# A gated linear attention with a mixer behind it: the attention runs one chunk ahead, the mixing is cut into small units, and the weights are loaded before the second batch

## The chip, the cores and the metric

The kernel runs on one core of one Trainium2 chip. The metric is the device time of one execution in microseconds (us); the kernel before took 243.04, 241.78 and 242.86 us in three runs, median 242.86. Engines are named as in the profile: PE (matrix unit; its weight loads stand apart as PEld), DVE (vector engine), ACT (activation engine), POOL (GpSimd), SP (the queue that issues plain DMAs). DMAs that convert a type are issued on POOL's queue.

## The reference

```python
# 4 batches, 8 heads, 768 steps, head width 48
f = 1 / (1 + exp(-f_logit))
for t in range(768):                                   # attention
    state = f[:, :, t, :, None] * state + k[:, :, t] (outer) v[:, :, t]
    y[:, :, t] = q[:, :, t] @ state
x = y.transpose(0, 2, 1, 3).reshape(4, 768, 384)
h  = relu(x^T @ w_tok1) @ w_tok2                       # 768 -> 256 -> 768, over the steps
u  = x + h^T
out = u + relu(u @ w_ch1) @ w_ch2                      # 384 -> 1536 -> 384, over the channels
```

All inputs and the output are fp32; both kernels use bf16 for matmuls and fp32 for sums.

## The kernel before, in words

**Attention.** The 768 steps of a batch are 6 chunks of 128. Per chunk (b, c) the log gates, split in two bf16 parts Lhi and Llo, are summed over the steps by two matmuls with a triangular matrix (`attn_front`, L154 and L156, 512 columns, into `ps_S`); eight matmuls of one column (L161, L163) give the sum over the whole chunk. ACT makes G = exp(-S), Gi = exp(S) and `glast`. DVE makes qh = q·G and kh = k·Gi. PE transposes both against an identity (L182 into `ps_AT[0]`, L184 into `ps_AT[1]`), ACT and DVE copy them to `qkT`, PE makes the scores of 8 heads (L191, into the same two banks), DVE masks them (`AmT`, L200, L201). PE makes y from `AmT` and v (L204) and adds qkT·state (L210); four matmuls of 96 columns (L215) make k·v of a pair of heads, of whose 2x2 blocks only the diagonal ones are used, so that DVE adds them to `state` in two instructions of 48 partitions, multiplies by `glast` and copies two blocks to `state_bd`. ACT writes y twice, as fp32 `x_nat` and bf16 `x_bf`.

**Mixing.** For a whole batch, in 6 slices: tok (w_tok1 12 matmuls, Relu to `h1T`; w_tok2 12 matmuls, DVE adds to `u_nat`, ACT casts to `u_bf`), utr (18 transposes, three DVE copies to `uT`), three slices of ch1 (24 units of 3 matmuls of 384 columns, each drained by a Relu on DVE or ACT to `zT`), and ch2 (6 units of 12 matmuls of 384 columns, one DVE add, one output DMA).

**Order.** The slices of batch b-1 are emitted inside the chunks of batch b, one slice a chunk, between the scores and the mask. The gates of batch b+1 (exp, ln, a copy to Lhi, a subtraction to Llo, each over the whole batch) are emitted one step a chunk. The mixing of batch 3 has no attention beside it. Eight PSUM tiles have fixed roles: five for attention (`ps_S`, `ps_AT` twice, `ps_y`, `ps_dg`), three rotate for the mixing. A scheduler then sets the order on each engine; it moves instructions across the places where they are written, and each engine runs its own list in order.

**Loads.** In this order: batch 0 chunk by chunk (f on SP; q, k, v on POOL's queue, 18 DMAs), batch 1 whole (q, k, v on POOL's queue, f on SP), the four weights (POOL's queue). Batch b+2 is loaded into the buffers of batch b when these are free.

Of the kernel before, what the change touches and what calls it, by code (L numbers as in the profile page):

```python
# [16 lines left out]
def kernel(  # L18
# [39 lines left out]
    w_ch1 = st([128, 3, DCH], BF16, "w_ch1")
    w_ch2 = st([128, 12, DM], BF16, "w_ch2")

    def load_weights():
        nc.gpsimd.dma_start(out=w_tok1, in_=moe_w_tok1.rearrange("(kt p) n -> p kt n", p=128))
        nc.gpsimd.dma_start(out=w_tok2, in_=moe_w_tok2.rearrange("(kt p) n -> p kt n", p=128))
        nc.gpsimd.dma_start(out=w_ch1, in_=moe_w_ch1.rearrange("(kt p) n -> p kt n", p=128))
        nc.gpsimd.dma_start(out=w_ch2, in_=moe_w_ch2.rearrange("(kt p) n -> p kt n", p=128))

    q_sb = [st([128, H, NCH, D], BF16, f"q_sb{i}") for i in range(2)]
    k_sb = [st([128, H, NCH, D], BF16, f"k_sb{i}") for i in range(2)]
    v_sb = [st([128, H, NCH, D], BF16, f"v_sb{i}") for i in range(2)]
# [4 lines left out]
    def load_batch_inputs(b, c0=0, c1=NCH):
        i = b % 2
        if (c0, c1) == (0, NCH):
            nc.gpsimd.dma_start(out=q_sb[i], in_=q[b].rearrange("h (c t) d -> t h c d", t=C))
            nc.gpsimd.dma_start(out=k_sb[i], in_=k[b].rearrange("h (c t) d -> t h c d", t=C))
            nc.gpsimd.dma_start(out=v_sb[i], in_=v[b].rearrange("h (c t) d -> t h c d", t=C))
            nc.sync.dma_start(out=f_sb[i], in_=f_logit[b].rearrange("h (c t) d -> t h c d", t=C))  # L80
# [11 lines left out]
    G = [st([128, H, 64], BF16, f"G{i}") for i in range(2)]
    Gi = [st([128, H, 64], BF16, f"Gi{i}") for i in range(2)]
    qh = [st([128, H, 64], BF16, f"qh{i}") for i in range(2)]
    kh = [st([128, H, 64], BF16, f"kh{i}") for i in range(2)]
    qkT = [st([128, 8, 128], BF16, f"qkT{i}") for i in range(2)]
    AmT = [st([128, 8, 128], BF16, f"AmT{i}") for i in range(2)]
    glast = st([128, HP], FP32, "glast")
    state = st([128, HP, D], FP32, "state")
    state_bd = st([128, HP, 2 * D], BF16, "state_bd")  # L100
    x_nat = [st([128, NCH, DM], FP32, f"x_nat{i}") for i in range(2)]
    x_bf = [st([128, NCH, DM], BF16, f"x_bf{i}") for i in range(2)]
# [6 lines left out]
    for tl in (*Lhi, *Llo):
        nc.vector.memset(tl[:, :, :, D:64], 0.0)  # L110
    nc.vector.memset(state_bd, 0.0)

    ps_S = pt([128, 512], FP32, "ps_S")
    ps_AT = [pt([128, 4, 128], FP32, f"ps_AT{p}") for p in range(2)]
    ps_y = pt([128, H, D], FP32, "ps_y")
    ps_dg = pt([128, HP, 2 * D + 1], FP32, "ps_dg")

    h1T = st([128, 2, DM], BF16, "h1T")
    u_nat = st([128, NCH, DM], FP32, "u_nat")
    u_bf = st([128, NCH, DM], BF16, "u_bf")  # L120
    uT = st([128, 3, S], BF16, "uT")
    zT = st([128, 12, S], BF16, "zT")
# [253 lines left out]
```

## Time and profile before

| What | Value |
|---|---|
| median of three runs | 242.86 us |
| the profiled execution's own time | 242.51 us |
| its span in the trace | 240.4 us |
| PE / PEld / DVE / ACT / POOL busy | 183.6 / 111.5 / 152.1 / 137.2 / 40.1 us |
| DMA | 19.93 MB, 91539 packets, 80896 of them under 512 B |
| MATMULs seen, 128x384 | ch1 288, ch2 288 |

The span is the time between the first and the last instruction seen; the execution's own time is 2.1 us longer. Shares over the whole span mix an early part, in which little runs but DMAs, with later parts in which PE is nearly always busy. The tables below are therefore cut at the first ch1 matmul of batch 0 and at the first w_tok1 matmul of batches 1, 2 and 3.

### The profile page before, as it was taken

The numbers are of one execution on the slowest core, as the hardware profiler recorded it, in microseconds if no ns is written. First come the engines' busy times: TensorE is split into PE (matmuls) and PEld (weight loads), VectorE is DVE, ScalarE is ACT, GpSimd is POOL, SyncE is SP. The second block draws the span as 40 slices with busy tenths as digits, with TensorE's granted clock in tenths as the row PEclk, the third lists the DMA queues.
The fourth block names the chain that finished last, engine by engine and source line by source line (L and its number), as shares of the span: only waits on it lengthen the run. The fifth ranks groups of instructions, "written<-read, shape, count | busy, mean of one in ns | idle before, by whom it ended". The sixth has DMA issues, their size and how long they took to land.

```text
span 240.4 us, 4273 instructions
## 1 busy us (share of the span) xinstructions
PE 183.6 (76%) x1673; PEld 111.5 (46%) x1688; DVE 152.1 (63%) x341; ACT 137.2 (57%) x262; POOL 40.1 (17%) x39
## 2 busy tenths in 40 slices
PE   0413376103858999999999999999999999989993
PEld 0201253001535555566565555666556556546661
DVE  4323769300965999995489998637999872444221
ACT  5479999900697765870376777008776710556300
POOL 9823910821302100150300000000000000000000
PEclk9999999999965999999999999999999999999999
DMA  8999999999999900099490000121000002100022
GB/s 113 147 185 151 163 158 137 174 144 198 208 182 137 103 3 0 3 85 174 135 104 0 3 1 3 65 100 35 0 3 0 3 33 102 64 0 0 8 107 85
DMA packets 91539, 19.93 MB, mean 83 GB/s; under 512 B 80896, under 2 KB 91136, under 8 KB 91520
## 3 DMA queue, kind: packets, MB, share of 16 engines
q0 software_dynamic: 77168, 10.23, 78.3%
q1 hardware_dynamic: 14352, 9.44, 18.4%
q8 instruction: 13, 0.21, 0.4%
q14 instruction: 6, 0.05, 0.1%
HBM read 25.17 MB, written 4.72 MB: 124 GB/s over the span
## 4 chain that ended last, share of the span: by engine, by line
PE 34%; DVE 26%; DMA 15%; issue 9%; ACT 8%; POOL 7%; DVEq 0%; POOLq 0%
DMA q_sb_77<-in_q_dram 6%; DMA w_tok_73<-in_moe_w_tok_dram 6%; PE ps_moe_135 L298 5%; PE ps_moe_133 L298 5%; PE ps_moe_134 L298 5%; PE ps_moe_133 L280 3%; DMA out_dram<-out_sb_132 3%; DVE zT L285 3%; PE ps_moe_134 L280 3%; PE ps_moe_135 L280 3%; DVE u_nat L256 2%; DVE qkT_98 L186 2%; DVE AmT_99 L200 2%; DVE uT L270 2%; DVE state L225 2%
## 5 line engine op out<-in xcount | busy, mean ns | idle before, releaser
L298 PEld LDWEIGHTS <-zT 128*128 128x128 bf16 x288 | 27.7, 98 | 18.3
L280 PEld LDWEIGHTS <-w_ch_75 128*128 128x128 bf16 x288 | 26.5, 97 | 19.9 <-issue 4.5
L280 PE MATMUL ps_moe_133<-uT,w_ch_75 128*128 128x384 bf16 x96 | 22.9, 325 | 1.4 <-DVE uT L270 0.5
L280 PE MATMUL ps_moe_135<-uT,w_ch_75 128*128 128x384 bf16 x96 | 22.6, 325 | 0.8 <-DVE zT L285 0.5
L280 PE MATMUL ps_moe_134<-uT,w_ch_75 128*128 128x384 bf16 x96 | 22.2, 325 | 0.5 <-DVE zT L285 0.3
L220 ACT ACTIVATE x_nat_105<-ps_y 128x384 f32<-128x384 f32 x12 | 6.0, 499 | 24.8 <-PE ps_y L210 24.2
L298 PE MATMUL ps_moe_134<-w_ch_76,zT 128*128 128x384 bf16 x96 | 17.3, 326 | 0.0
L200 DVE TENSOR_TENSOR AmT_100<-ps_AT_122,tri_bf 128x512 bf16<-128x512 f32 x12 | 8.3, 688 | 14.2 <-PE ps_AT_123 L191 14.0
L298 PE MATMUL ps_moe_135<-w_ch_76,zT 128*128 128x384 bf16 x96 | 17.1, 326 | 0.0
L298 PE MATMUL ps_moe_133<-w_ch_76,zT 128*128 128x384 bf16 x96 | 17.1, 326 | 0.0
L287 ACT ACTIVATE zT<-ps_moe_134 128x384 bf16<-128x384 f32 x22 | 10.9, 496 | 8.0 <-PE ps_moe_134 L280 7.8
L161 PE MATMUL ps_dg<-ones_bf,Lhi_85 128*128 128x1 bf16 x40 | 3.5, 166 | 13.5 <-ACT Lhi_85 L143 6.7
L287 ACT ACTIVATE zT<-ps_moe_135 128x384 bf16<-128x384 f32 x22 | 11.0, 500 | 4.9 <-PE ps_moe_135 L280 4.8
L220 ACT ACTIVATE x_nat_104<-ps_y 128x384 f32<-128x384 f32 x12 | 5.8, 486 | 13.9 <-PE ps_y L210 13.9
L247 PE MATMUL ps_moe_134<-x_bf_106,w_tok_73 128*128 128x384 bf16 x6 | 2.5, 452 | 14.1 <-DMA w_tok_73<-in_moe_w_tok_dram 12.2
L247 PEld LDWEIGHTS <-w_tok_73 128*128 128x128 bf16 x48 | 4.6, 105 | 17.9 <-DMA w_tok_73<-in_moe_w_tok_dram 12.4
L287 ACT ACTIVATE zT<-ps_moe_133 128x384 bf16<-128x384 f32 x20 | 10.0, 500 | 4.3 <-PE ps_moe_133 L280 4.2
L224 DVE TENSOR_TENSOR state<-state,ps_dg 48x192 f32<-48x192 f32 x20 | 6.8, 342 | 8.5 <-ACT qkT_98 L185 4.9
L257 ACT ACTIVATE u_bf<-u_nat 128x384 bf16<-128x384 f32 x24 | 11.0, 519 | 1.8 <-DVE u_nat L256 1.6
L200 DVE TENSOR_TENSOR AmT_99<-ps_AT_122,tri_bf 128x512 bf16<-128x512 f32 x12 | 8.2, 685 | 6.0 <-PE ps_AT_123 L191 5.7
L175 ACT ACTIVATE glast<-ps_dg 128x4 f32<-128x4 f32 x20 | 3.6, 178 | 14.1 <-DVE state L227 12.7
L191 PE MATMUL ps_AT_122<-qkT_97 48*128 48x128 bf16 x48 | 5.1, 232 | 7.3 <-ACT qkT_97 L185 5.5
(149 smaller groups left out, 470.3 us busy)
## 6 DMA issues: line engine op xcount, KB each, us to landing
out_dram<-out_sb_131 SPq DMA_DIRECT2D x12, 192.0 KB, 1.9
out_dram<-out_sb_132 SPq DMA_DIRECT2D x12, 192.0 KB, 1.9
f_sb_83<-in_f_logit_dram SPq DMA_DIRECT2D x6, 192.0 KB, 5.7
q_sb_78<-in_q_dram POOLq DMA_DIRECT2D x2, 576.0 KB, 12.6
k_sb_80<-in_k_dram POOLq DMA_DIRECT2D x2, 576.0 KB, 18.2
v_sb_82<-in_v_dram POOLq DMA_DIRECT2D x2, 576.0 KB, 11.6
w_ch_75<-in_moe_w_ch_dram POOLq DMA_DIRECT2D x1, 1152.0 KB, 20.3
w_ch_76<-in_moe_w_ch_dram POOLq DMA_DIRECT2D x1, 1152.0 KB, 24.9
```

The lines of the kernel that those rows point to most:

```text
L186: nc.vector.tensor_copy(qkT[i][:, 4:8, :], ps_AT[1])
L191: nc.tensor.matmul(ps_AT[par][:, hp, :], lhsT=qkT[i][rows, 4 + hp, :], rhs=qkT[i][rows, hp, :], start=True, stop=True)
L200: nc.vector.tensor_tensor(AmT[i][:, 0:4, :], ps_AT[0], tb4, ALU.mult)
L220: nc.scalar.activation(x_nat[ib][:, c, :], yflat, AF.Copy, bias=0.0, scale=1.0)
L224: nc.vector.tensor_tensor(state[0:D], state[0:D], ps_dg[0:D, :, 0:D], ALU.add)
L225: nc.vector.tensor_tensor(state[64:64 + D], state[64:64 + D], ps_dg[64:64 + D, :, D:2 * D], ALU.add)
L247: nc.tensor.matmul(pm[:, 0:DM], lhsT=w_tok1[:, kt, rt * 128:(rt + 1) * 128], rhs=x_bf[ib][:, kt, :], start=(kt == 0), stop=(kt == NCH - 1))
L257: nc.scalar.activation(u_bf[:, stt, :], u_nat[:, stt, :], AF.Copy, bias=0.0, scale=1.0)
L280: nc.tensor.matmul(pm[:, 0:384], lhsT=w_ch1[:, kt, cc * 128:(cc + 1) * 128], rhs=uT[:, kt, th * 384:(th + 1) * 384], start=(kt == 0), stop ...
L285: nc.vector.tensor_scalar(dst, pm[:, 0:384], 0.0, None, ALU.max)
L287: nc.scalar.activation(dst, pm[:, 0:384], AF.Relu, bias=0.0, scale=1.0)
L298: nc.tensor.matmul(pm[:, 0:DM], lhsT=zT[:, kt, tt * 128:(tt + 1) * 128], rhs=w_ch2[:, kt, :], start=(kt == 0), stop=(kt == 11))
```

## The change

The kernel is written anew with the same arithmetic; what differs:

- **Attention ahead.** `attn_chunk` becomes `front` (gate sums to qh, kh), `scores` (transposes to AmT), `update` (state) and `readout` (y). Step n emits scores of chunk n+1, update of n, front of n+2, readout of n.
- **Mixing units.** The mixing of a batch is 44 units (2 tok1, 6 tok2, 6 utr, 24 ch1, 6 ch2) with weights; a credit spreads them evenly over four places in each of the 6 steps of the next batch.
- **PSUM.** Mixing takes 3 tiles of tag "mix", attention takes 5 rotating tiles of tag "att".
- **Compact state.** Eight matmuls of 48 columns write k·v of each head to its own partitions, so that `state` is one add and one multiply over 128 partitions; `state` and `state_bd` are doubled. S has 384 columns in place of 512, with the chunk sums in the same bank.
- **Engines.** Lhi is a second Ln on ACT, not a copy. Beyond batch 0, Llo, `x_bf` (now cast from `x_nat`), `u_bf` and the two `state_bd` copies go to POOL; in batch 0 they are on DVE. `uT` is copied by ACT, one block of steps at a time (6 of 128x384). 10 of 24 ch1 units drain on DVE, against 8 before. One activation table set is loaded at the start.
- **Loads.** f of batch 0, then q, k, v of batch 0 by chunks; the weights; then f, q, k, v of batch 1, f on POOL's queue too.

```diff
-        nc.tensor.matmul(ps_S, lhsT=tri_bf, rhs=hi_c.rearrange("t h dd -> t (h dd)"), ...)
+        nc.tensor.matmul(Sv, lhsT=tri_bf, rhs=Lhi[i][:, c, :, 0:D], start=True, stop=False)   # Sv = pS[:, 0:384]
...
-            for hp in range(HP):
-                nc.tensor.matmul(ps_dg[:, hp, 0:2 * D], lhsT=kb[:, hp, :],
-                                 rhs=v_sb[ib][:, 2 * hp:2 * hp + 2, c, :], ...)
+        for h in range(H):
+            hp, par = h // 2, h % 2
+            nc.tensor.matmul(pd[par * 64:par * 64 + 64, hp * D:(hp + 1) * D], lhsT=kh[j][:, h, :],
+                             rhs=v_sb[i][:, h, c, :], start=True, stop=True)
...
+            nc.vector.tensor_tensor(s, state[1 - j], pdv, ALU.add)
+            nc.vector.tensor_tensor(s, s, g, ALU.mult)
+        eng = nc.gpsimd if b else nc.vector
+        eng.tensor_copy(state_bd[j][0:D, :, 0:D], s[0:D])
+        eng.tensor_copy(state_bd[j][64:64 + D, :, D:2 * D], s[64:64 + D])
...
-        nc.scalar.activation(x_bf[ib][:, c, :], yflat, AF.Copy, bias=0.0, scale=1.0)
+        (nc.gpsimd if b else nc.vector).tensor_copy(x_bf[i][:, c, :], x_nat[i][:, c, :])
...
-                nc.scalar.activation(u_bf[:, stt, :], u_nat[:, stt, :], AF.Copy, bias=0.0, scale=1.0)
+            (nc.gpsimd if b else nc.vector).tensor_copy(u_bf[:, tt, :], u_nat[i][:, tt, :])
...
+        nc.scalar.activation(fb, fb, AF.Exp, bias=0.0, scale=-1.0)
+        nc.scalar.activation(Lhi[i][:, c0:c1, :, 0:D], fbc, AF.Ln, bias=1.0, scale=1.0)
+        nc.scalar.activation(fb, fb, AF.Ln, bias=1.0, scale=1.0)
+        eng = nc.gpsimd if b else nc.vector
+        eng.tensor_tensor(Llo[i][:, c0:c1, :, 0:D], fbc, Lhi[i][:, c0:c1, :, 0:D], ALU.subtract)
...
-    load_batch_inputs(1)
-    load_weights()
+    for w, src in ((w_tok1, moe_w_tok1), (w_tok2, moe_w_tok2), (w_ch1, moe_w_ch1), (w_ch2, moe_w_ch2)):
+        nc.gpsimd.dma_start(out=w, in_=src.rearrange("(kt p) n -> p kt n", p=128))
+    load_f(1, nc.gpsimd)
+    load_qkv(1)
...
+        def mix():
+            nonlocal credit
+            credit += per_step                  # the sum of the units' weights / 24
+            while prev and credit >= prev[0][0] / 2:
+                w, fn = prev.pop(0)
+                credit -= w
+                fn()
+        if n + 1 < len(steps):
+            scores(*steps[n + 1])
+        mix()
+        update(b, c)
+        mix()
+        if n + 2 < len(steps):
+            front(*steps[n + 2])
+        mix()
+        readout(b, c)
+        mix()
+        if b + 1 < B and 1 <= c <= 3:
+            gates(b + 1, 2 * (c - 1), 2 * c)
```

**POOL's queue, at the end of the first loads.** Before (buffers 77, 79, 81 hold batches 0 and 2; 78, 80, 82 batches 1 and 3):

```order
L89 DMA v_sb_81<-in_v_dram 128x8x48
L77 DMA q_sb_78<-in_q_dram 128x48x48
L78 DMA k_sb_80<-in_k_dram 128x48x48
L79 DMA v_sb_82<-in_v_dram 128x48x48
L62 DMA w_tok_73<-in_moe_w_tok_dram 128x6x256
L63 DMA w_tok_74<-in_moe_w_tok_dram 128x2x768
L64 DMA w_ch_75<-in_moe_w_ch_dram 128x3x1536
L65 DMA w_ch_76<-in_moe_w_ch_dram 128x12x384
L77 DMA q_sb_77<-in_q_dram 128x48x48
```

With the change (78, 80, 82 hold q, k, v of batches 0 and 2; 79, 81, 83 and f_sb_85, Lhi_87, Llo_89 belong to batches 1 and 3):

```order
L278 DMA w_tok_75<-in_moe_w_tok_dram 128x2x768
L278 DMA w_ch_76<-in_moe_w_ch_dram 128x3x1536
L278 DMA w_ch_77<-in_moe_w_ch_dram 128x12x384
L110 DMA f_sb_85<-in_f_logit_dram 128x48x48
L118 DMA q_sb_79<-in_q_dram 128x48x48
L118 DMA k_sb_81<-in_k_dram 128x48x48
L118 DMA v_sb_83<-in_v_dram 128x48x48
L131 TENSOR_TENSOR Llo_89<-f_sb_85,Lhi_87 128x16x48 x3
L118 DMA q_sb_78<-in_q_dram 128x48x48
L118 DMA k_sb_80<-in_k_dram 128x48x48
L118 DMA v_sb_82<-in_v_dram 128x48x48
L207 CAST state_bd_106<-state_104 48x4x48
```

The weights moved ahead of batch 1, f of batch 1 came in from SP's queue, and POOL now has work of the attention between its DMAs: the three parts of Llo of batch 1 stand behind the issue of v of batch 1, and the first state copy of batch 1 behind the loads of batch 2.

**DVE, where the first mixing begins** (batch 0's tok and utr, beside the first chunks of batch 1). Before:

```order
L256 TENSOR_TENSOR u_nat<-x_nat_104,ps_moe_133 128x384
L256 TENSOR_TENSOR u_nat<-x_nat_104,ps_moe_134 128x384
L256 TENSOR_TENSOR u_nat<-x_nat_104,ps_moe_135 128x384
L201 TENSOR_TENSOR AmT_99<-ps_AT_123,tri_bf 128x512
L230 CAST state_bd<-state 48x4x48
L270 COPY uT<-ps_moe_133 128x768
L270 COPY uT<-ps_moe_134 128x768
```

With the change:

```order
L202 TENSOR_TENSOR state_104<-pd,gl_102 128x192
L228 TENSOR_TENSOR u_nat_113<-x_nat_108,pm 128x384
L150 TENSOR_TENSOR qh_94<-q_sb_79,G_90 128x8x48
L229 CAST u_bf<-u_nat_113 128x384
L151 TENSOR_TENSOR kh_96<-k_sb_81,Gi_92 128x8x48
L228 TENSOR_TENSOR u_nat_113<-x_nat_108,pm 128x384 x2
L229 CAST u_bf<-u_nat_113 128x384 x2
```

DVE gained the casts to `u_bf` in this batch and lost the copies to `uT`; in the later batches the casts are POOL's. The rows of `u_nat` now stand around the qh and kh of chunk (1, 2). On PE the first matmul of chunk (1, 0), with Lhi of batch 1, stands ahead of the readout of chunk (0, 4).

More of the change, by code (lines that the diff above doesn't have):

```diff
@@ L92 @@
[L92 to L100, printed above, removed]
@@ L104, in blk @@
+    h1T = st([128, 2, DM], BF16, "h1T")
+    u_nat = two([128, NCH, DM], FP32, "u_nat")
+    u_bf = st([128, NCH, DM], BF16, "u_bf")
+    uT = st([128, 3, S], BF16, "uT")
+    zT = st([128, NCC, S], BF16, "zT")
+    out_sb = two([128, DM], FP32, "out_sb")
+    for tl in (*Lhi, *Llo):
+        nc.vector.memset(tl[:, :, :, D:64], 0.0)
+    for tl in (*qh, *kh):
+        nc.vector.memset(tl[:, :, D:64], 0.0)
+    for tl in state_bd:
+        nc.vector.memset(tl, 0.0)
     def blk(ap3):
         return ap3.rearrange("t (hp par) dd -> t hp (par dd)", par=2)
-    for tl in (*qh, *kh, *G, *Gi):
-        nc.vector.memset(tl[:, :, D:64], 0.0)
@@ L109 @@
[L109 to L122, printed above, removed]
```

386 lines of the change are left out of this document (171 added, 215 removed).

## The prediction

> **What bounds the kernel now.** I read the page's slices first, then busy time by stage, the chain of waits, the longest waits, the DMA issues.
>
> ```profile
> span 240.4 us, 4273 instructions
> PE   0413376103858999999999999999999999989993
> PEclk9999999999965999999999999999999999999999
> DMA  8999999999999900099490000121000002100022
> ```
>
> For a third of the span PE has little to do and the DMAs are full; then it turns round. Cut at the first ch1 matmul of batch 0 (83.9 us) and at the first tok1 matmul of batches 1, 2 and 3:
>
> ```profile
> core 0: us, PE busy (x) PEld busy (x) DVE busy (x) ACT busy (x) POOL busy (x), PEclk, DMA share, GB/s
> 0.00:83.90 83.90, 36.81 (x348) 22.80 (x353) 44.22 (x98) 59.46 (x82) 33.50 (x36) 0.94 2.20 157
> 83.90:120.30 36.40, 34.98 (x343) 21.13 (x346) 29.73 (x66) 19.22 (x45) 6.55 (x3) 1.00 0.76 67
> 120.30:163.15 42.85, 41.25 (x409) 25.57 (x413) 33.57 (x80) 23.41 (x57) 0.09 (x1) 1.00 0.33 38
> 163.15:205.20 42.05, 40.43 (x393) 24.71 (x394) 32.43 (x76) 22.56 (x54) 0.00 (x0) 1.00 0.08 30
> 205.20:240.44 35.24, 30.11 (x187) 17.29 (x184) 12.17 (x24) 12.52 (x26) 0.00 (x0) 1.00 0.11 40
> ```
>
> From 83.9 us to 205.2 us PE is busy 96% of the time; DVE has about 9 us free per batch and ACT 19, so relief for them there buys little. By spacing, a batch's 168 matmuls of 384 columns take 27.3 us (ch2 below: 1.95 us for twelve), 18 transposes 1 us and six chunks about 11: 39.4 us, so some 3 us of 42 are small waits. The last stage, with 5 us of PE idle, is mixing alone. The first stage is the loose one. Its chain of waits and its longest wait say why:
>
> ```profile
> 30.70 11.26 issue
> 41.96 1.73 POOL v_sb_82 L79
> 44.17 13.95 DMA w_tok_73<-in_moe_w_tok_dram
> 58.16 0.82 PE ps_moe_134 L247 x2
> ...
> 205.23 0.81 PE ps_moe_134 L247 x5
> ...
> 214.06 0.49 PE ps_moe_135 L280 x3
> ...
> 232.74 1.95 PE ps_moe_134 L298 x12
> ```
>
> ```profile
> PE ps_moe_134 L247 <- DMA w_tok_73<-in_moe_w_tok_dram: 12.2, 1, 12.2
> ```
>
> The scheduler put two tok1 matmuls of batch 0 among its last chunks, and w_tok1 stood behind batch 1 in POOL's queue. So PE's first wait is for a load, and the sum is made stage by stage.
>
> **First stage: the loads.** They run without a gap, so I count bytes.
>
> ```profile
> 7.10 2.21 SPq L80 DMA_DIRECT2D f_sb_84<-in_f_logit_dram  x1
> 23.23 0.70 SPq L80 DMA_DIRECT2D f_sb_83<-in_f_logit_dram  x1
> 37.82 0.69 SPq L80 DMA_DIRECT2D f_sb_84<-in_f_logit_dram  x1
> ```
>
> ```profile
> 46.41 1.04 POOL L65 DMA_DIRECT2D w_ch_76<-in_moe_w_ch_dram  x1
> ...
> w_ch_76<-in_moe_w_ch_dram POOLq DMA_DIRECT2D x1, 1152.0 KB, 24.9
> q_sb_78<-in_q_dram POOLq DMA_DIRECT2D x2, 576.0 KB, 12.6
> ```
>
> ```profile
> 14.00:19.00 5.00, 1.29 (x16) 0.81 (x16) 1.29 (x2) 4.97 (x4) 0.90 (x2) 1.00 1.41 186
> 72.00:76.00 4.00, 3.09 (x38) 2.20 (x38) 1.99 (x4) 2.89 (x6) 0.00 (x0) 0.50 2.89 144
> ```
>
> The last weight landed at 46.4 + 24.9 = 71.3 us. By then f of all four batches (SP issued batches 2 and 3 at 23.23 and 37.82, as soon as buffers were free), q, k, v of batches 0 and 1, the weights and about 2 us of q of batch 2 had moved. With the change v of batch 1 comes last of this set, and f of batch 3 waits until the gates of batch 1 are made: 1.18 MB at 186 GB/s (a stretch with an f load in flight) is 6.3 us. So v lands at 71.3 - 6.3 - 2 = 63 us; at 144 GB/s (only q, k, v loads) the 590 KB of v, k and q take 4.1 us each: k at 59, q at 55, f at 51. How fast f goes on POOL's queue no row shows: 4 us if packets count as in q, 8 us at 144 GB/s; I keep 6 (ends -2, +2). Batch 0, f of batch 2 and w_tok1 are 4.5 MB, 29 us at this stage's 157 GB/s, so the 12.2 us wait goes, but a new one takes its place: PE has the first matmul of chunk (1, 0) ahead of the last readouts of batch 0.
>
> Three paths meet there. (a) kh needs k: 59 us. (b) ACT makes the gates of batch 1 in nine passes of 768 elements after f:
>
> ```profile
> 5.58 0.52 ACT L140 ACTIVATE f_sb_83<-f_sb_83 128x384 f32<-128x384 f32 x1
> 17.31 1.80 ACT L140 ACTIVATE f_sb_83<-f_sb_83 128x1920 f32<-128x1920 f32 x1
> ```
>
> 0.52 + 384 x 0.83 ns = 0.84 us each, 7.6 us, with one y copy 59 us. (c) Llo of batch 1 stands on POOL behind the issue of v. The third whole-batch load was issued 11.3 us after the second was (the "issue" row above), so I let v's issue wait until q has landed (55), and 2.2 us more as k and v took: 57. POOL's price for Llo has no row; the nearest:
>
> ```profile
> masks.py:66 POOL TENSOR_SCALAR_AFFINE_SELECT tri_bf<-tri_bf 128x128 bf16<-128x128 bf16 x1 | 0.3, 282 | 0.0
> L360 POOL MEMSET const-float32-0.0<- 128x1 f32 x1 | 0.1, 99 | 0.2 <-issue 0.2
> L146 DVE TENSOR_TENSOR Llo_88<-f_sb_84,Lhi_86 128x2304 bf16<-128x2304 f32 x2 | 5.1, 2556 | 0.0
> L257 ACT ACTIVATE u_bf<-u_nat 128x384 bf16<-128x384 f32 x24 | 11.0, 519 | 1.8 <-DVE u_nat L256 1.6
> ```
>
> DVE's rate (2556/2304 = 1.1 ns an element) gives 0.85 us for 768, POOL's select (183 ns more for 127 more elements, 1.4 ns each) 1.2 us, twice that 2.3 us. I take 1.5, since this has two inputs: 58.5 us. The Trainium skill (GPSIMD Engine Reference, 3.1) puts a two-input elementwise instruction at about 2.6 cycles an element at 1.2 GHz: by that page an estimate of 1.7 us, which would make 58.7; no row here shows it.
>
> So the gate sums come at 59, qh at 60.5, the transposes of (1, 0) at 61. From there to the first ch1 lie the scores of (1, 0) and (1, 1) and tok2 and utr of batch 0. The like stretch before, from the transposes of (0, 5) to ch1:
>
> ```profile
> 68.21 0.60 PE L182 MATMUL ps_AT_122<-ident,qh_94 128*128 128x128 bf16 x4
> ...
> 83.92 0.78 PE L280 MATMUL ps_moe_133<-uT,w_ch_75 128*128 128x384 bf16 x2
> ```
>
> 15.7 us. Now DVE does six `u_nat` (0.55 each) and six `u_bf` there beside two chunks, about 10 us in a row, and the three 0.55 us `uT` copies are gone; I take 16. First ch1 at **77 us** for 83.9 (ends 72 and 84).
>
> **Batch 0's mixing (36.4 us).** Attention is one transposition and score ahead: -1.2 us. The clock costs:
>
> ```profile
> 34.07 0.49 PE L210 MATMUL ps_y<-state_bd,qkT_98 128*128 128x96 bf16 x4
> 34.37 0.63 PE L182 MATMUL ps_AT_122<-ident,qh_93 128*128 128x128 bf16 x4
> 87.24 0.34 PE L204 MATMUL ps_y<-v_sb_82,AmT_100 128*128 128x48 bf16 x7
> 87.42 0.33 PE L210 MATMUL ps_y<-state_bd,qkT_98 128*128 128x96 bf16 x4
> 87.59 0.33 PE L280 MATMUL ps_moe_135<-uT,w_ch_75 128*128 128x384 bf16 x1
> 66.00:72.00 6.00, 3.20 (x32) 2.05 (x30) 4.17 (x11) 5.95 (x9) 0.00 (x0) 0.61 1.83 183
> ```
>
> The same four matmuls start 0.30 us before their successor early and 0.17 us at 87 us: PE ran at about half rate while it had little work (0.61 granted at 66 to 72). Before, it was fast by the first ch1; now ch1 follows 25 us of thin work. The Trainium skill (TensorE: Matmul & The Clock Gate, Part 1) says a full clock comes after about 3.4 us of busy time; these rows agree that it comes late. I charge 2.5 us (0 to 5, the half of 10 us at half rate). Behind it nothing is late: the first state copy of batch 1 on POOL comes at about 79 us, after q, k, v of batch 2, and its reader on PE follows 21 ch1 matmuls. Sum 36.4 - 1.2 + 2.5 = 37.7.
>
> **Batches 1 and 2 (42.85 and 42.05).** Twelve ch2 matmuls take 1.95 us, 0.42 ns a column, so two matmuls of 384 for 512 columns save 0.11 us a chunk. Seven matmuls of 48 columns take 0.18 us (87.24 to 87.42), four of 96 take 0.17: eight for four cost 0.03. That is -0.5 us a batch, all that PE itself gains. DVE's two state adds become one and its two copies leave, `uT` too; ACT loses `x_bf` and `u_bf` and gains `uT`: both lie under PE, I take -0.1 (ends -2.5, nearly all small waits; +4, casts on POOL at twice 0.64 in series). 42.2 and 41.5.
>
> **Last stage (35.24).** From the first tok1 to ch1 took 8.8 us. `x_bf` of the last chunk lies under a ch2 unit. Casts on POOL at 0.1 + 384 x 1.4 ns = 0.64 us follow `u_nat` at 0.55, and ch1 needs only three blocks of `uT`: tok1 1.95 us, `h1T` and handover 0.6, then 5.0 to the sixth transposed block: 7.6, so -1.2. 34.0.
>
> **Sum:** 77 + 37.7 + 42.2 + 41.5 + 34.0 = 232.4 us of span. The profiled execution took 2.1 us more than its span (242.51 against 240.4) and lies 0.35 us under the median: 234.5 us.
>
> **Rivals.** (1) *Better in the steady part*: smaller units and rotating banks take half of the 3 us of small waits in each of three stages, and ch1 starts at 72 us: 234.5 - 4.5 - 5 = 225 us. For it: DVE was busy 33 of 42 us, in an order that PE must wait for. Against: PE is at 96% as it is. 25%. (2) *POOL's casts are slow.* In batches 1 to 3 the six `u_bf` are in series ahead of utr. Each us over 0.64 costs 6 us a batch where nothing covers it, 18 in all; the 8.3 us gain is gone at 1.1 us a cast, and at 1.6 us the time is 252. For it: two of the four price rows are of small fills; ACT's 0.52 and POOL's 0.64 speak against. 14%. (3) *DVE and POOL hold each other up.* POOL is busy 16 us a batch (ten state copies at 0.37, twelve casts, three Llo); were each of 17 DVE instructions with two SBUF inputs to wait 0.4 us (the rest of a POOL instruction, long ones being hit more often) in 16 of 42 cases, DVE gets 2.6 us more a batch, on the path 8 in all: 242.5, no change. The Trainium skill (SBUF — State Buffer, Who interferes with whom) says such pairs exclude each other; no run here shows it, and DVE's 9 free us should take it. 8%. (4) *f of batch 3 collides with v of batch 1*: SP sends it when the third Llo is read, about 62 us; if v is not through by then, it is 6 us late: 240.5. 8%. That the reorder does nothing is in (3).
>
> **Numbers.** Forecast 234.5 with 45% (its own range 228 to 241). The range of 8 in 10, 223 to 246, takes in the better case and the lower half of the slow casts. This kernel's runs differ by 0.5%, so less is no change: faster 45 + 25 + 7 (of rival 4) = 77%, no change 8%, slower 15%.
>
> **What would show it.** Right: no wait of tok1 for w_tok1; first ch1 at 72 to 80 us; PE's first wait of over 5 us ends in k, gates or Llo of batch 1; batches at 41 to 43 us; no wait of utr on POOL over 2 us. Wrong: POOL casts over 1.1 us, PE idle over 3 us at utr and the granted clock under 1.00 after 85 us; or a first stage over 83 us.

## The result, and the profile after

The changed kernel took 234.58 us (median of 235.0, 234.28, 231.15 and 234.88), the kernel before 242.69 us beside it: ratio 0.960, interval 0.948 to 0.971. (Ratios here and below leave out executions more than 1.5% above the fastest of their kernel: here 234.88 and 235.0, so that the profiled execution, the longest of the four and 3.85 us above the shortest, is not among those of the ratio.) The prediction was 234.5. The profiled execution took 235.0 us, 2.0 more than its span. From its page, and cut as the prediction cut it (first ch1, then the first tok1 of batches 1, 2, 3; the columns are those of the prediction's table):

```profile
span 233.0 us, 4447 instructions
...
PE   0125778501379669999999999999999999999994
PEclk9999999999999997999999999999999999999999
DMA  8999999999999990009996000121000021100022
```

```profile
0.00:79.99 79.99, 38.55 (x392) 23.51 (x393) 43.29 (x100) 44.45 (x90) 40.17 (x40) 1.00 2.01 158
79.99:117.31 37.32, 34.92 (x351) 21.81 (x351) 26.20 (x48) 19.54 (x44) 22.69 (x25) 0.95 0.99 75
117.31:159.34 42.03, 41.67 (x446) 26.43 (x444) 29.39 (x62) 21.40 (x51) 10.20 (x24) 1.00 0.36 44
159.34:198.88 39.54, 39.19 (x402) 24.61 (x399) 25.68 (x54) 19.04 (x44) 9.41 (x22) 1.00 0.09 31
198.88:233.00 34.12, 29.97 (x187) 17.54 (x185) 11.97 (x23) 10.34 (x22) 2.83 (x6) 1.00 0.12 41
```

| stage | before | predicted | after |
|---|---|---|---|
| to the first ch1 | 83.90 | 77 | 79.99 |
| to the first tok1 of batch 1 ("MoE 0") | 36.40 | 37.7 | 37.32 |
| of batch 2 ("MoE 1") | 42.85 | 42.2 | 42.03 |
| of batch 3 ("MoE 2") | 42.05 | 41.5 | 39.54 |
| last | 35.24 | 34.0 | 34.12 |

The sum was right to 0.6 us, the parts less so: the first stage is 3.0 us longer than predicted, MoE 2 2.0 shorter. In the two full stages PE's idle time fell from 1.60 and 1.62 us to 0.36 and 0.35. The list of PE's waits, and the seam between batch 0 and batch 1 in the timeline (start, length, engine and line; in brackets the idle time before and what ended it):

```profile
PE pS L138 <- ACT Lhi_87 L128: 8.8, 1, 8.8
PE pm L219 <- DVE x_bf_110 L187: 6.4, 3, 5.9
...
PE pm L242 <- DVE zT L246: 2.3, 1, 2.3
...
PE pm L219 <- DMA w_tok_74<-in_moe_w_tok_dram: 1.1, 1, 1.1
```

```profile
51.74 1.58 ACT L127 ACTIVATE f_sb_85<-f_sb_85 128x768 f32<-128x768 f32 x2 [7.99 <-DMA f_sb_85<-in_f_logit_dram]
55.42 2.21 POOL L118 DMA_DIRECT2D v_sb_83<-in_v_dram  x1 [1.10 <-issue]
57.37 3.73 DVE L187 CAST x_bf_110<-x_nat_108 128x384 bf16<-128x384 f32 x1 [9.91 <-ACT x_nat_108 L186]
57.64 4.95 POOL L131 TENSOR_TENSOR Llo_89<-f_sb_85,Lhi_87 128x768 bf16<-128x768 f32 x3
61.15 0.80 PE L219 MATMUL pm<-x_bf_110,w_tok_74 128*128 128x384 bf16 x2 [5.94 <-DVE x_bf_110 L187]
```

The wait of 12.2 us for w_tok1 is now 1.1 us. In its place PE waits 8.8 us for the gates of batch 1, whose f landed at 51.7, and then 5.9 us for an `x_bf` of *batch 0*: ACT writes its `x_nat` late, at 57.3, between the gates, and then this cast, 0.36 us elsewhere, takes 3.73 us on DVE while POOL issues v's load and runs Llo. The same returns behind the first ch1:

```profile
81.80 5.06 POOL L131 TENSOR_TENSOR Llo_88<-f_sb_84,Lhi_86 128x768 bf16<-128x768 f32 x3
82.02 1.63 DVE L205 TENSOR_TENSOR state_105<-state_105,gl_103 128x192 f32<-128x192 f32 x1
83.57 1.79 DVE L150 TENSOR_TENSOR qh_95<-q_sb_79,G_91 128x384 bf16<-128x384 bf16 x1
85.28 1.79 DVE L151 TENSOR_TENSOR kh_97<-k_sb_81,Gi_93 128x384 bf16<-128x384 bf16 x1
87.59 0.65 PE L242 MATMUL pm<-uT,w_ch_76 128*128 128x384 bf16 x3 [2.30 <-DVE zT L246]
...
88.00:92.00 4.00, 4.00 (x27) 2.12 (x25) 1.89 (x5) 1.80 (x4) 3.29 (x5) 0.57 0.03 6
```

Three DVE instructions of 0.36 us take as long as a pass of Llo, ch1 waits 2.3 us for a Relu queued behind them, and the granted clock falls to 0.57 for the next 4 us (last row, from the busy time by stretches). These are the only DVE instructions in the trace that are far above the usual time of their kind; all lie beside Llo or a DMA issue on POOL. So two questions were tried: was the order of the loads the gain, as predicted, and do DVE and POOL hold each other up?

### The profile page after: what moved, and what is told of

Same layout as the page of the kernel before. It is cut to its first block, busy times and chain, and to the rows that moved or that the text cites. A ratio compares the mean times of both kernels' runs of the same rounds, so it can differ in the third digit from the quotient of the medians.

```text
span 233.0 us, 4447 instructions
## 1 busy us (share of the span) xinstructions
PE 184.3 (79%) x1768; PEld 113.9 (49%) x1768; DVE 136.5 (59%) x283; ACT 114.8 (49%) x250; POOL 85.3 (37%) x115
## 4 chain that ended last, share of the span: by engine, by line
PE 60%; DMA 18%; ACT 7%; DVE 7%; POOL 6%; issue 1%; DVEq 0%; ACTq 0%; POOLq 0%
PE pm L242 20%; PE pm L253 18%; DMA f_sb_85<-in_f_logit_dram 13%; PE pm L226 4%; DMA k_sb_80<-in_k_dram 4%; PE pm L219 3%; ACT uT L236 3%; PE pq L158 2%; DMA out_dram<-out_sb_119 2%; PE pk L162 2%; ACT f_sb_85 L127 2%; DVE x_bf_110 L187 2%; POOL q_sb_78 L120 2%; PE py L178 1%; PE pd L196 1%; PE pS L139 1%
## 5 line engine op out<-in xcount | busy, mean ns | idle before, releaser
L242 PE MATMUL pm<-uT,w_ch_76 128*128 128x384 bf16 x288 | 55.1, 330 | 2.4 <-DVE zT L246 2.3
L253 PE MATMUL pm<-w_ch_77,zT 128*128 128x384 bf16 x288 | 50.6, 326 | 0.0
L248 ACT ACTIVATE zT<-pm 128x384 bf16<-128x384 f32 x56 | 27.5, 492 | 23.9 <-PE pm L242 23.8
L246 DVE TENSOR_SCALAR zT<-pm 128x384 bf16<-128x384 f32 x40 | 21.2, 552 | 7.8 <-PE pm L242 7.5
L146 ACT ACTIVATE G_90<-pS 128x384 bf16<-128x384 f32 x12 | 5.9, 488 | 15.2 <-PE pS L145 12.5
L226 PE MATMUL pm<-h1T,w_tok_75 128*128 128x384 bf16 x48 | 12.2, 354 | 0.7 <-ACT h1T L221 0.5
L236 ACT CAST uT<-pm 128x384 bf16<-128x384 f32 x24 | 10.2, 488 | 3.6 <-PE pm L234 3.5
L163 DVE CAST qkT_98<-pk 128x512 bf16<-128x512 f32 x12 | 8.3, 689 | 5.8 <-PE pk L162 5.8
L146 ACT ACTIVATE G_91<-pS 128x384 bf16<-128x384 f32 x12 | 5.8, 485 | 10.0 <-PE pS L145 10.0
L131 POOL TENSOR_TENSOR Llo_89<-f_sb_85,Lhi_87 128x768 bf16<-128x768 f32 x6 | 9.9, 1671 | 0.1
L234 PE MATMUL pm<-ident,u_bf 128*128 128x128 bf16 x72 | 7.5, 218 | 3.1 <-ACT uT L236 1.8
```

The lines of the kernel that those rows point to most:

```text
L131: eng.tensor_tensor(Llo[i][:, c0:c1, :, 0:D], fbc, Lhi[i][:, c0:c1, :, 0:D], ALU.subtract)
L146: nc.scalar.activation(G[j].rearrange("t h d -> t (h d)"), Sv, AF.Exp, bias=0.0, scale=-1.0)
L163: nc.vector.tensor_copy(qkT[j][:, 4:8, :], pk.rearrange("p (a t) -> p a t", a=4))
L226: nc.tensor.matmul(pm[:, 0:DM], lhsT=w_tok2[:, kt, tt * 128:(tt + 1) * 128], rhs=h1T[:, kt, :], start=(kt == 0), stop=(kt == 1))
L236: nc.scalar.copy(uT[:, :, tt * 128:(tt + 1) * 128], pm[:, 0:DM].rearrange("p (m t) -> p m t", m=3))
L242: nc.tensor.matmul(pm[:, 0:384], lhsT=w_ch1[:, kt, cc * 128:(cc + 1) * 128], rhs=uT[:, kt, th * 384:(th + 1) * 384], start=(kt == 0), stop ...
```

## The experiments

Ratios are to the kernel before, beside it on the same chip, with 95% intervals. "First ch1" and the stages are from each profiled run, one of each kernel.

**Llo on DVE.** The theory is that POOL's Llo holds DVE up.

```diff
-        eng = nc.gpsimd if b else nc.vector
+        eng = nc.vector
         eng.tensor_tensor(Llo[i]...)
```

> The changed kernel with one edit: Llo of batches 1 to 3 (L131) goes from POOL to DVE. In the trace of the changed kernel x_bf (L187) of batch 0 took 3.73 us and the state's mult, qh and kh 1.63, 1.79 and 1.79 us while POOL issued v's load or ran Llo. Theory A (DVE and POOL hold each other up): these four fall back to their usual length, about 0.3 to 0.4 us; against that DVE gets 3 more subtractions for each batch, estimated at 1.7 us each or less, by POOL's row. The first ch1 starts 1 to 2 us earlier than 79.99, the wait of 2.30 us of ch1 on zT at 87.59 and the stretch at half clock after it go, and the time falls by 3 to 5 us against the changed kernel, to some 230 to 232 us. Theory B (the long DVE instructions have another cause, or DVE has no room): the three subtractions on DVE take the place of the hold-up, and the time stays within 1.5 us of the changed kernel's 234.6 us, or rises.

232.18 us, 0.956 [0.953, 0.960]: by time alone not told from the changed kernel, whose interval holds it. The stages say more:

```profile
78.64:112.94 34.30, 33.51 (x350) 21.24 (x348) 24.23 (x51) 19.50 (x44) 14.69 (x19) 1.00 1.11 83
```

MoE 0 takes 34.30 us in place of 37.32, at full clock, without the wait of ch1 on zT; the state's multiply, qh and kh are back at their usual length. The first stage gained only 1.35 us, to 78.64:

```profile
60.67 0.36 DVE L151 TENSOR_TENSOR kh<-k_sb,Gi 128x384 bf16<-128x384 bf16 x1 [2.74 <-DMA k_sb<-in_k_dram]
...
61.82 1.45 DVE L187 CAST x_bf<-x_nat 128x384 bf16<-128x384 f32 x1
```

kh now waits for k (the prediction's path a), and `x_bf` still takes 1.45 us, with q of batch 2 being issued on POOL from 60.89 to 63.11. Theory A for MoE 0; in the first stage another wait was next.

**The copies back on DVE.**

```diff
-        (nc.gpsimd if b else nc.vector).tensor_copy(x_bf[i]...)     # u_bf, state_bd likewise
+        nc.vector.tensor_copy(x_bf[i]...)
```

> The changed kernel with the copies x_bf (L187), u_bf (L229) and state_bd (L207, L208) of batches 1 to 3 on DVE, as for batch 0; Llo stays on POOL. In the changed kernel x_bf takes 0.50 us on POOL and each half of state_bd 0.34. Theory A (in the steady stages the matmuls set the pace and POOL's copies lie beside them): the stages of MoE 1 and 2 and the last stage move by less than 0.5 us each, and the time stays within 1.5 us of 234.6 us. Theory B (rival 3 of the prediction, DVE and POOL hold each other up in the steady part also): DVE is freed of waits, and each of the stages of MoE 1 and 2 gets 1 us or more shorter, the time 231 to 232 us. Theory C (DVE becomes the bound): each of them gets 1 us or more longer, the time 237 us or more.

245.14 us, 1.010 [1.005, 1.016]: theory C, and more of it. MoE 1:

```profile
122.80:168.09 45.29, 43.51 (x446) 26.86 (x444) 35.47 (x85) 21.55 (x51) 0.26 (x1) 0.96 0.33 40
```

DVE has 6.1 us more to do there and the stage is 3.3 us longer; MoE 2 2.8, MoE 0 5.0 (granted clock 0.92), the last 1.1. The profiled execution was 2.3 us above its median, so these sizes are rough. The change needs POOL's copies (0.50 us for `x_bf`, 0.34 for half a `state_bd`, where 0.64 and 0.37 were predicted): with them on DVE the rewritten kernel is no faster than the one before.

**The old load order in the changed kernel.**

```diff
+    load_qkv(1)
+    load_f(1, nc.sync)
     for w, src in (...): nc.gpsimd.dma_start(out=w, ...)
-    load_f(1, nc.gpsimd)
-    load_qkv(1)
```

> The changed kernel with the loads of batch 1 ahead of the mixing weights again, as in the kernel before (q, k, v on POOL's queue, f on SP's); the rest of the change stays. Theory A (the order of the loads is worth what the prediction's stage 1 says): the first tok1 has to wait for its weight again, the first ch1 of MoE 0 starts at 83 to 85 us in place of 79.99, and the time goes to 237 to 240 us. Theory B (the gain of stage 1 came from the attention's being ahead and not from the loads): the first ch1 stays at 79 to 81 us and the time within 1 us of 234.6 us.

230.33 us, 0.943 [0.936, 0.950]. Both theories fell. With the weights *behind* batch 1 the first ch1 starts at 77.26, 2.7 us earlier than with the change's order:

```profile
47.37 4.90 POOL L131 TENSOR_TENSOR Llo<-f_sb,Lhi 128x768 bf16<-128x768 f32 x3
53.01 2.10 PE L219 MATMUL pm<-x_bf,w_tok 128*128 128x384 bf16 x6 [11.11 <-DMA w_tok<-in_moe_w_tok_dram]
61.11 0.61 PE L158 MATMUL pq<-ident,qh 128*128 128x128 bf16 x4 [0.98 <-DVE qh L150]
...
77.26 0.97 PE L242 MATMUL pm<-uT,w_ch 128*128 128x384 bf16 x5
```

PE waits 11.1 us for w_tok1, nearly as long as before, but to 53.0 us, not 58.2, and the Llo of batch 1 with its hold-up lies inside that wait. The transposes of (1, 0) start at 61.1, in the changed kernel at 63.4. MoE 1 and 2 are the changed kernel's to 0.01. MoE 0 is 34.56 us, only 0.3 above that with Llo on DVE, although Llo of batch 2 runs on POOL there and holds DVE up again:

```profile
81.49 1.79 DVE L151 TENSOR_TENSOR kh<-k_sb,Gi 128x384 bf16<-128x384 bf16 x1
```

Here ch1 waits 1.2 us for zT, not 2.3, and the granted clock stays at 1.00 from 77 to 93 us. So the same hold-up can cost little; what it costs depends on what waits behind it.

**The mixing at one place.**

```diff
-        mix(); update(b, c); mix(); front(*steps[n + 2]); mix(); readout(b, c); mix()
+        update(b, c); front(*steps[n + 2]); mix(); mix(); mix(); mix(); readout(b, c)
```

> The changed kernel with the four groups of mixing units of a step put at one place, behind the front, in place of one group each behind the scores, the update, the front and the readout; same instructions, same load order, same banks. Theory A (being one chunk ahead is what keeps PE fed, and the spreading of the units matters little): the stages of MoE 1 and 2 (42.03 and 39.54 us) stay within 1 us each and the time within 2 us of 234.6 us. Theory B (the spreading fills the waits between the pieces of attention): scores, update and readout of a chunk stand one after the other, PE waits for ACT and DVE between them, some 1 us per chunk, 6 us per stage, and the time goes to 245 us or more.

237.47 us, 0.974 [0.968, 0.979]; its lower end lies below the changed kernel's upper one (0.971). Its profiled execution was 2.3 us above its median, so no stage of it is compared. Theory B is out (245 or more); theory A's 2 us were passed by 0.9 in the medians, and since the intervals overlap, whether the spreading is worth anything is not settled.

**f of batch 3 late, in the kernel before.** w_tok1 came 5 us earlier with the old order than in the kernel before, which sent f of batch 3 at 37.8 us.

```diff
-            nc.sync.dma_start(out=f_sb[i], in_=f_logit[b]...)
+            (nc.gpsimd if b == 3 else nc.sync).dma_start(out=f_sb[i], in_=f_logit[b]...)
```

> The kernel before with one edit: f of batch 3 goes on POOL's queue (L80), behind q, k, v of batch 3, and so comes late. In the trace of the kernel before SP issued it at 37.82 us and k, v of batch 1 and w_tok1, which were in flight or behind, landed at 52.55, 56.55 and 58.12 us. With the changed kernel's other parts but the old load order, f of batch 3 was issued at 52.36 us, these three landed at 45.04, 50.45 and 52.97 us, the first ch1 started at 77.26 us and the time was 230.3 us. Theory A (a good part of what the change gained in stage 1 is that f of batch 3 comes late, since the gates of batch 1 are made later; nothing of it needs the weights ahead): w_tok1 lands at about 53 us, the first ch1 starts at 78 to 80 us in place of 83.9, and the time is 237 to 239.5 us. Theory B (f of batch 3 was hidden, and stage 1 gained by the attention's order): the first ch1 stays at 83 to 85 us and the time within 1 us of 242.9 us.

246.88 us, 1.019 [1.012, 1.025], longer, the time of neither theory; yet the first ch1 is 6.7 us earlier:

```profile
53.14 0.82 PE L247 MATMUL ps_moe<-x_bf,w_tok 128*128 128x384 bf16 x2 [6.86 <-DMA w_tok<-in_moe_w_tok_dram]
...
77.20 0.32 PE L280 MATMUL ps_moe<-uT,w_ch 128*128 128x384 bf16 x1
...
87.14 2.12 ACT L137 ACTIVATE f_sb<-f_sb 128x2304 f32<-128x2304 f32 x1 [4.36 <-DMA f_sb<-in_f_logit_dram]
...
89.70 1.76 PE L280 MATMUL ps_moe<-uT,w_ch 128*128 128x384 bf16 x5 [3.85 <-ACT zT L287]
```

Theory A holds for the first stage: the old kernel with only this edit has its first ch1 where the changed one with the old load order has it (77.20 and 77.26). The time is lost behind it: the scheduler had put the gates of batch 3 early in ACT's list, ACT waits there for f, Relus queue behind, PE waits 3.85 us and runs at a granted 0.61 and 0.54 from 88 to 96 us; MoE 0 to 2 take 44.75, 44.99 and 42.07 us.

**The weights ahead, in the kernel before.**

```diff
-    load_batch_inputs(1)
     load_weights()
+    load_batch_inputs(1)
```

> The kernel before with one edit: the four weights ahead of batch 1 in POOL's queue (f of batch 1 stays on SP's). Theory A (as the run with the old load order in the changed kernel speaks: the weights ahead do not pay, since batch 1 then comes some 14 us later, 2.6 MB at about 186 GB/s, and PE waits for k of batch 1 in place of w_tok1): the wait of 12.2 us for w_tok1 goes, a wait of like length for k or kh of batch 1 comes, the first ch1 starts at 82 to 88 us and the time is 241 to 247 us. Theory B (the prediction: the weights' place is the gain): the first ch1 starts at 77 us or earlier and the time is 236 us or less.

239.73 us, 0.987 [0.983, 0.990], first ch1 at 81.22: between the theories. Here f of batch 1 stayed on SP's queue and landed at 21.7 us. In the changed kernel it stands behind the weights and lands at 51.7, and the gates and Llo follow it; that this is why the same move pays here and not there is argued, not tried alone.

**w_tok1 alone ahead of batch 1**, the other weights behind it, f on SP.

```diff
+    nc.gpsimd.dma_start(out=w_tok1, ...)
+    load_qkv(1)
+    load_f(1, nc.sync)
-    for w, src in ((w_tok1, ...), (w_tok2, ...), (w_ch1, ...), (w_ch2, ...)): ...
-    load_f(1, nc.gpsimd)
-    load_qkv(1)
+    for w, src in ((w_tok2, ...), (w_ch1, ...), (w_ch2, ...)): ...
```

> The changed kernel with another load order: w_tok1 alone ahead of batch 1, then q, k, v of batch 1 on POOL's queue and f on SP's, then the other three weights. Theory A (PE needs w_tok1 first, then batch 1's first chunk, and ch1 only 16 us later; so what is late in either order is gone): tok1 does not wait, k lands at about 47 us, v at 52, w_ch1 at 62 to 64; Llo on POOL stands behind the issue of the weights and comes at about 51 us; the transposes of (1, 0) start at 52 to 55 us in place of 63.4, the first ch1 at 68 to 71, and the time is 221 to 225 us. Theory B (the rest of stage 1 is bound by the work on DVE and ACT or by the low clock, not by loads): the first ch1 stays at 75 us or later, the time 228 us or more.

233.83 us, 0.961 [0.956, 0.966], first ch1 at 78.91: theory B by the numbers. k, v and w_ch1 came about as theory A had them (46.5, 52.3, 60.1 us), but w_tok1 landed at 38.3 us, behind f of batch 2 on SP's queue, so that tok1 still waited 7.9 us for it, and the work behind was late too:

```profile
43.36 2.28 POOL L118 DMA_DIRECT2D v_sb<-in_v_dram  x1 [5.74 <-issue]
43.81 2.70 DVE L208 CAST state_bd<-state 48x192 bf16<-48x192 f32 x1
46.55 1.66 DVE L151 TENSOR_TENSOR kh<-k_sb,Gi 128x384 bf16<-128x384 bf16 x1
48.12 4.96 POOL L131 TENSOR_TENSOR Llo<-f_sb,Lhi 128x768 bf16<-128x768 f32 x3
48.13 1.86 DVE L187 CAST x_bf<-x_nat 128x384 bf16<-128x384 f32 x1
```

Three DVE instructions take 6.2 us there in place of 1.0, and PE waits 4.0 us for this kh.

**The same, with Llo on DVE.**

```diff
     # as the run before, and
-        eng = nc.gpsimd if b else nc.vector      # Llo
+        eng = nc.vector
```

> As the run before, with Llo of batches 1 to 3 on DVE (0.95 us each there when it was tried alone, 1.67 on POOL). Theory A (Llo waits behind DMA issues on POOL, and holds DVE up when it runs there): the transposes of (1, 0) start 3 to 5 us earlier than with Llo on POOL, at 47 to 50 us, as soon as k has landed; the first ch1 waits for its weight or starts at 64 to 66 us, the time is 217 to 221 us. Theory B (the weights' landing is next in line): w_ch1 lands at 62 to 66 us and w_ch2 at 71 to 75, and the gain over Llo on POOL is under 2 us.

227.85 us, 0.937 [0.933, 0.941], first ch1 at 72.53: 6.0 us less by this one edit, with intervals well apart. That is what Llo's place on POOL costs in this load order, and the hold-up is only a part of it. The sums of the gates of chunk (0, 5), behind the three held DVE instructions, start 3.35 us earlier (48.31 for 51.66). The rest comes at chunk (1, 0), whose sums over Llo start 5.8 us earlier; here the run before and this one:

```profile
60.29 0.80 PE L219 MATMUL pm<-x_bf,w_tok 128*128 128x384 bf16 x2 [0.96 <-DVE x_bf L187]
60.89 0.52 PE L139 MATMUL pS<-Llo,tri_bf 128*128 128x384 bf16 x1
```

```profile
55.08 0.53 PE L139 MATMUL pS<-Llo,tri_bf 128*128 128x384 bf16 x1
```

With Llo on POOL two tok1 matmuls stand ahead of these sums in PE's list and wait for an `x_bf`, though Llo was done at 53.1 us; on DVE they stand behind. MoE 0 gains nothing (35.85 us, 35.22 with Llo on POOL). w_ch1 landed at 64.8 us, as theory B had it, but the gain was not under 2 us. The expected first ch1 at 64 to 66 was missed:

```profile
PE pm L219 <- DMA w_tok<-in_moe_w_tok_dram: 8.1, 1, 8.1
```

tok1 waited for w_tok1, which landed at 38.4 us, behind f of batch 2 on SP's queue.

**f of batches 2 and 3 on POOL's queue, in the changed kernel.**

```diff
-                load_f(b + 2, nc.sync)
+                load_f(b + 2, nc.gpsimd)
```

> The changed kernel with one edit: f of batches 2 and 3 goes on POOL's queue (behind q, k, v of the batch before) in place of SP's. In the changed kernel SP issued f of batch 2 at 16.50 us and it landed at 28.71; loads on POOL's queue that were issued at 16 to 18 us landed at 28 to 30. Theory A (a whole f on SP's queue takes the DMAs from what PE waits for; it costs its bytes, 1.18 MB at 186 GB/s, 6.3 us): the weights, f, q, k, v of batch 1 land some 6 us earlier (f at 45.5, k at 54.5), the first ch1 starts at 73 to 75 us in place of 79.99 and the time is 228 to 230 us, if f of batch 2, which now comes at about 70 us, makes ACT wait nowhere. Theory B (PE's chain through batch 0's chunks on DVE and ACT is what is late, f of batch 2 or not): k lands earlier, but the first ch1 stays at 78 us or later, the time 232 us or more.

230.31 us, 0.950 [0.947, 0.953]; w_tok1 landed at 26.5 (31.2), f of batch 1 at 46.6 (51.7), k at 55.8 (60.8), the first ch1 at 74.56. Theory A but for 0.3 us of the total, though the interval overlaps the changed kernel's: a whole f on SP's queue costs the others 5 us. MoE 0 (36.81 us) now has ACT wait 2.1 us for f of batch 3.

**All three edits.**

```diff
     # w_tok1 first and Llo on DVE, and
-                load_f(b + 2, nc.sync)
+                load_f(b + 2, nc.gpsimd)
```

> w_tok1 ahead of batch 1, Llo on DVE, and f of batches 2 and 3 on POOL's queue behind the weights. With the first two edits alone tok1 waited 8.1 us for w_tok1, which landed at 38.4 us behind f of batch 2 (SP, 16.7 to 31.1 us), and f of batch 3 (SP, 42.2 us) ran beside v and the weights; the first ch1 was at 72.5 us and the time 227.85 us. Theory A (both f loads are in the way): w_tok1 lands at 30 to 32 us, w_ch1 at 53 to 56, the first ch1 starts at 65 to 67 us, and f of batch 2 lands at 68 to 70, ahead of its gates; the time is 220 to 223 us. Theory B (ACT, in whose list the gates of batch 2 stand, waits for f of batch 2, as it waited 4.4 us for f of batch 3 when that came late in the kernel before): the first ch1 is early, but the stage of MoE 0 is longer than 36 us by 3 us or more, and the time is 224 us or more.

225.80 us, 0.931 [0.928, 0.935], neither theory: w_tok1 landed at 31.5, but the first ch1 is at 74.86. The stall of theory B is there, ahead of ch1 and not behind it:

```profile
68.09 0.84 ACT L127 ACTIVATE f_sb<-f_sb 128x768 f32<-128x768 f32 x1 [7.53 <-DMA f_sb<-in_f_logit_dram]
...
72.03 1.12 PE L234 MATMUL pm<-ident,u_bf 128*128 128x128 bf16 x9 [9.32 <-ACT uT L236]
```

ACT stood at the gates of batch 2 until their f landed, with the `uT` copies behind.

**w_ch2 behind f of batch 2.**

```diff
                 load_f(b + 2, nc.gpsimd)
+                if b == 0:
+                    nc.gpsimd.dma_start(out=w_ch2, ...)       # taken out of the first loop
```

> As the run before, with w_ch2 behind f of batch 2, so that this f lands some 5 us earlier (about 63 us) and w_ch2 later (about 70 us). Theory A (f of batch 2 is needed ahead of w_ch2, which is read 16 us or more behind the first ch1): no wait of ACT for f of batch 2, none of ch2 for w_ch2, and the time is 219 to 222 us. Theory B (neither is late): the same as the run before within 1 us.

224.88 us, 0.927 [0.925, 0.930]. The first ch1 is at 69.31, 5.6 us earlier, but the next f does the same in MoE 0 (38.19 us):

```profile
86.85 0.84 ACT L127 ACTIVATE f_sb<-f_sb 128x768 f32<-128x768 f32 x1 [2.19 <-DMA f_sb<-in_f_logit_dram]
...
88.13 1.12 PE L242 MATMUL pm<-uT,w_ch 128*128 128x384 bf16 x3 [1.73 <-ACT zT L248]
```

**f of batch 3 ahead of w_ch2 too.**

```diff
                 if b == 0:
+                    load_f(2, nc.gpsimd)
+                    load_f(3, nc.gpsimd)
                     nc.gpsimd.dma_start(out=w_ch2, ...)
-                load_f(b + 2, nc.gpsimd)
```

> As the run before, with f of batch 3 also ahead of w_ch2 and of q, k, v of batch 2, behind f of batch 2. In the run before ACT, whose list is in order, waited 2.2 us at 86.85 for f of batch 3, behind it lay the Relus of ch1, PE waited 1.7 us and then ran at about half clock (0.57 from 88 to 92 us), and the stage of MoE 0 took 38.2 us where two others took 34.3 to 34.8. Theory A (that one wait and the clock behind it are the 3.5 us): f of batch 3 lands at about 66 us, w_ch2 at 72, the stage of MoE 0 takes 34 to 35.5 us, the first ch1 stays at 69 to 70, and the time is 220.5 to 222.5 us. Theory B (the wait only moves: w_ch2 or q of batch 2 is late in its place): the time stays within 1 us of 224.9 us.

223.78 us (five runs), 0.921 [0.918, 0.924]: faster than both kernels, 1.3 us above what theory A allowed. Behind the first ch1 (69.82) ACT waits for no f; ahead of it, it still waits 4.6 us for f of batch 2. f of batch 3 landed at 66.9 and w_ch2 at 72.4, and MoE 0 fell by 2.0 us to 36.14. What is left of it over the 34.3 us of the first experiment lies, for the most part, at its start, where PE is busy all the time at a granted 0.57:

```profile
70.00:74.00 4.00, 4.00 (x31) 1.98 (x30) 3.96 (x8) 2.64 (x5) 0.00 (x0) 0.57 2.46 154
```

## Why the prediction was right, and where it was wrong

That the time was right to 0.6 us of span is in part luck: two errors met (the first stage 3.0 us long, MoE 2 2.0 short), and a cause that was wrong gave a sum that was nearly right. (The sum also leaves out the 0.35 us that it names between the profiled execution and the median.)

- **What removes the wait for w_tok1** ("so the 12.2 us wait goes"): it went, but having the weights first was not the gain. With the old order back, no run reached the 237 to 240 us of theory A: they took 227.21 to 232.85 us, with the order of the change 231.15 to 235.0. The intervals overlap a little, so that the new order costs time is likely and not shown. What moved the first stage is in the prediction's own byte count, where it was one term among several: f of batch 3 comes later, "1.18 MB at 186 GB/s is 6.3 us". Alone, in the kernel before, that moved w_tok1 by 5.0 us and the first ch1 by 6.7, to where the changed kernel with the old order has it. The prediction did not ask what each half of its load term was worth alone.
- **The first stage at 77 us.** The landings were right to 2 us: f 51.7 (51 predicted), k 60.8 (59), v 64.9 (63); so were the gates (59.0, predicted 59) and Llo's price (1.65 us, taken 1.5). The step that failed is "three paths meet there": there is a fourth, DVE's `x_bf` of batch 0, held 3.73 us by POOL's issue and Llo, in front of two tok1 matmuls that stand in PE's list ahead of the sums of chunk (1, 0). The transposes of (1, 0) came at 63.4, not 61, and the stretch from there took 16.5 us (16). With Llo on DVE, kh was there at 61.0, as soon as k had landed, but the first ch1 only at 78.64: of the 3.0 us, that edit gives back 1.35. What makes up the rest is not shown; an `x_bf` still held beside an issue (1.45 us) lies in it.
- **MoE 0 at 37.7.** 37.32 measured, by another sum. The 2.5 us for a cold clock were not paid as charged: four transposes take 0.61 us at 67.8 us and 0.42 at 74.4, so PE was at its full rate before ch1 (the granted clock reads 1.00 on both sides and does not show this), and the clock fell later, behind the hold-up. With Llo on DVE the stage is 34.30, which is -2.1 where -1.2 was predicted, and no clock term. The count of score matmuls fits: the stages of MoE 0, 1 and 2 held 48, 40 and 48 before and hold 32, 48 and 40 now, so two chunks left MoE 0, not one. The clock term is real elsewhere: the last experiment pays, by estimate, about 1.7 us of it (0.43 of 4 us).
- **MoE 1 and 2 at 42.2 and 41.5.** MoE 1 was right to 0.2, with its parts off: PE's busy time did not fall by 0.5 but rose by 0.4 (41.25 to 41.67; one chunk's scores came in), and the small waits, put at -0.1, fell by 1.2. MoE 2 is 2.0 shorter than predicted: "attention is one transposition and score ahead: -1.2" was put into MoE 0 alone, but where the attention ends the lead is gained too: this stage has 8 of 48 score matmuls less, and 1.2 us of waits less.
- **Last stage**: 34.0 predicted, 34.12 measured.
- **Rivals.** Of rival 1, the small waits came in part (1.2 us in each of the two full stages, 1.5 put); ch1 at 72 us did not. Slow casts (2) did not come: 0.50 us against the 1.1 at which the gain goes. Rival 4's condition was met, f of batch 3 was issued at 62.7 us and v of batch 1 landed at 64.9, but v was 2 us late, not 6. Rival 3, DVE and POOL hold each other up, was given 8% and is real, at other instructions: not the short copies of the steady stages (42.03 and 39.54 us, with Llo off POOL 42.10 and 39.54), but Llo and the DMA issues at the seam. In MoE 0 the profiled runs are 3.0 us apart with Llo on POOL and on DVE (37.32 and 34.30), the drop of the clock included; with w_tok1 first the edit is worth 6.0 us, of which about 3.4 lie at held instructions; with the old loads the hold-up is there and MoE 0 takes 34.56. The prediction said that no run showed it; the trace of the kernel before did, in its timeline, with a cast that takes 0.25 us elsewhere:

```profile
26.11 2.24 POOL L77 DMA_DIRECT2D q_sb_78<-in_q_dram  x1
...
26.37 2.06 DVE L229 CAST state_bd<-state 48x192 bf16<-48x192 f32 x1
```

  The Trainium skill (SBUF — State Buffer, Who interferes with whom) says that DVE and GpSimd share a pair of SBUF ports as an exclusive lock: a DVE instruction in a two-port mode, as a cast can be, and a GpSimd one block each other, whoever issues first keeping the pair for its whole instruction, and a DVE instruction with two SBUF inputs contends with a GpSimd instruction that reads SBUF. These rows agree: 2.06 us for a cast beside an issue of 2.24, and above 1.79 us for qh beside a pass of Llo.
- **"Relief there buys little"** was wrong in one direction: DVE's 9 free us a batch did not take the copies, which cost about 3 us in MoE 1 when they came back.

What stays open: what the spreading of the units is worth, why the same weights-first order pays in the old kernel, and what the shortest execution of the changed kernel (231.15 us) did otherwise, since no trace of it was kept.

## What to carry to other kernels

Where a load is late, list all that moves ahead of it, on other queues too, and price each alone: here a whole f on SP's queue cost 5 us, and the reordering that looked like the point was not what brought the gain. Where a chain passes through them, do not count DVE's casts within SBUF at their usual length beside POOL's DMA issues, nor its instructions with two SBUF inputs beside long two-input work on POOL; look through the old trace for the longest of each kind, not its mean. A late load ahead of an engine's list blocks all behind it, so an early transfer of what the scheduler has placed early can be worth more than one of what looks needed first.

## What the runs showed of the hardware

- Beside Llo on POOL, DVE instructions with two SBUF inputs were held: qh, kh and the state's multiply from 0.36 to 1.6 to 1.8 us, about one pass of Llo (1.63 to 1.75); in the 14 traces together 16 of 17 that began in a pass. Beside a load's issue on POOL they were not: 164 began while an issue still had most of their usual length to run, and 163 kept that length, in the changed kernel this kh:

```profile
62.54 2.26 POOL L118 DMA_DIRECT2D q_sb_78<-in_q_dram  x1
63.40 0.36 DVE L151 TENSOR_TENSOR kh_96<-k_sb_81,Gi_92 128x384 bf16<-128x384 bf16 x1
```

  The one exception is the kh of the run with w_tok1 first (46.55 to 48.21 us, the issues ended at 48.11); what held it is open.
- DVE's casts within SBUF, usually 0.25 to 0.36 us, were held beside both, up to 3.73 us; of 63 that began beside an issue, 35 took over one and a half times their usual length.
- DVE instructions that read PSUM kept their length (`qkT` 0.69 us beside Llo and beside issues).
- A pass of Llo takes 0.95 us on DVE and 1.65 on POOL.
- In the changed kernel and two experiments (f of batch 3 late, w_ch2 behind f of batch 2) a wait of PE of 1.7 to 3.9 us amid ch1 was followed by 4 to 8 us at a granted clock of 0.54 to 0.61; a wait of 1.2 us amid ch1, with the old load order, was not (1.00).
- A POOL load issued 0.9 us after another landed 6.9 us after it (28.22 and 21.33), with a whole f from SP's queue in between.
